# Retention and two feed-forward networks on one core: head tiles by pair, one weight piece ahead, ACT's table loaded first

## The chip, the cores and the metric

The kernel runs on one core of a Trainium2 chip. The time is device microseconds of one execution. Five engines work side by side, each on its own queue of instructions in order: PE multiplies matrices (PEld is its weight load), DVE and ACT do elementwise work, POOL does little here, and SP issues the transfers. An instruction that waits holds up everything behind it on its own engine.

## What is computed

The reference, cut to what matters. Four batches of eight heads go through a causal, decaying linear attention ("retention"), and the 2304 tokens that result through two networks.

```python
def _attn_ref(q, k, v):                      # 4 x 8 x 576 x 64
    scores = scale * np.matmul(q, k.transpose(0, 1, 3, 2))
    gamma = 1.0 - 2.0 ** (-5.0 - np.arange(H, dtype=np.float32))
    Dmat = np.where(rel >= 0, gamma[:, None, None] ** rel[None, :, :], 0.0)
    return np.matmul(scores * Dmat[None], v)

def _moe_ref(x, w1, w2, w3, w_out):          # x 2304 x 512
    return ((x @ w1) * (x @ w2) @ w3) @ w_out

def _moe2_ref(x, w_in, w_out, alpha):
    h = x @ w_in
    g = np.maximum(h, 0.0) + alpha * np.minimum(h, 0.0)
    return g @ w_out
```

## The kernel before

**Stages.** The retention of batch 0 comes first ("the heads"). Then the products of the first network, a = x @ w1 and b = x @ w2, run by blocks of 512 tokens, and the retention of the batches 1 to 3 is slipped in between them. Folded weights, the second product, the second network's hidden layer and its output follow; PE runs through those with few pauses, and no line of the change is in them.

**Retention.** Heads are taken in four pairs. A batch has one tile `qk` (queries and keys of all four pairs) and one tile `kv` (keys and values by chunk). `prep` (L246) scales the keys of a pair on ACT, two instructions a pair (L250). A step then handles one chunk of 128 tokens: PE makes the state product `st` (L272) and the scores `sc` (L276), DVE masks the scores (`rt`, L280) and carries the state `S` (L284 to L288), PE makes the output `o` from state and scores (L302, L310), DVE scales it (`xs`, L317), and ACT and DVE split it into a high and a low part, `xh` and `xl` (L169, L170), which the network multiplies. The last, half chunk has its own lines (L261, L263). Batch 0 is computed as two halves, pairs 0 and 1 (`r0`) and pairs 2 and 3 (`r1`), whose steps alternate in a list written out by hand (L380).

**Weights.** The weights come as float64 and are converted piece by piece by `Weights.tick` (L118), one stage a tick for each piece: ACT takes out two fields (L93, L94), DVE builds the float32 value from them in four instructions (L103, L104, L106, L108), ACT rounds it (L112), and DVE makes the rest (L116). `load_until` issues the transfers; five tiles `raw` hold pieces that are on their way. The heads tick at every second step, six times in all.

**Block 0 and batch 1.** An `ab_unit` (L401) does the two products of one column chunk: twelve matmuls (here called a unit) into `ps`, `cycle()`, twelve more, `cycle()`. A cycle runs the postponed work (`flush`), then steps of the next batch's retention at a given rate, then one tick. Before, batch 1's retention starts in the second of four `ab_unit`s and runs 7/6 steps a cycle. Block 1's first unit needs `xh` and `xl` of batch 1's chunk 3.

**Transfers.** SP issues all transfers in the order of the program. Batch 1's `qk` and `kv` go into the same two tiles as batch 0's, so each is one transfer, issued when PE has done with the heads (L391).

Of the kernel before, what the change touches and what calls it, by code (L numbers as in the profile page):

```python
# [7 lines left out]
F32 = mybir.dt.float32  # L8
# [8 lines left out]
P = 128  # L17
B, H, S, D = 4, 8, 576, 64
NPAIR = H // 2
NT, DM, DF1, DF2 = B * S, 512, 1024, 2048  # L20
CH = 128
# [114 lines left out]
def retention_moe_kernel(ctx: ExitStack, tc, qk, kv, w_out1, w3t, w12, w_in, w_out2, alpha, c_row, c_pair, out):  # L136
# [17 lines left out]

    idle = tmp.tile([P, 512], I32, tag="b", name="idle", bufs=2).bitcast(BF16)
    nc.vector.memset(idle, 0.0)

    later = []

# [77 lines left out]
    class Retention:  # L237
# [7 lines left out]

        def prep(self):  # L246
            for p in self.pairs:
                k = kvt[self.b][:, p]
                for j in range(2):
                    nc.scalar.activation(k[:, 4 * j:4 * j + 4], k[:, 4 * j:4 * j + 4], AF.Copy,  # L250
                                         scale=kd[:, 2 * p + j:2 * p + j + 1])

        def scores(self, c):
            b, n = self.b, self.n
            sc = self.psum["sc"].tile([P, 2, 512], F32, tag="sc", name=f"sc{b}_{c}")
            q, k, v = qkt[b][:, :, 0], qkt[b][:, :, 1], kvt[b]
            if c == NCH - 1:
                rt = self.rt[c] = attn.tile([P, NPAIR, 64], F32, tag="rte", name=f"rte{b}")[:, 0:n]
                for m, p in enumerate(self.pairs):
                    for pp in HEADS:  # L260
                        nc.tensor.matmul(sc[pp, 0, m * 64:(m + 1) * 64], k[pp, p, 512:S], q[pp, p, 512:S],  # L261
                                         start=True, stop=True, skip_group_check=True)
                later.append(lambda: nc.vector.tensor_tensor(  # L263
                    out=rt, in0=sc[:, 0, 0:64 * n].rearrange("p (n i) -> p n i", n=n), in1=mtail[:, self.ps],
                    op=ALU.mult))
                return
            i0 = c * CH
            rt = self.rt[c] = attn.tile([P, 2, NPAIR, CH], F32, tag="rt", name=f"rt{b}_{c}", bufs=2)[:, :, 0:n]
            st = self.psum["st"].tile([P, NPAIR, D], F32, tag="st", name=f"st{b}_{c}")[:, 0:n]
            for m, p in enumerate(self.pairs):  # L270
                for j, pp in enumerate(HEADS):
                    nc.tensor.matmul(st[pp, m], v[:, p, 4 * j + c], v[:, p, 8 + 4 * j + c],  # L272
                                     start=True, stop=True, skip_group_check=True)
            for m, p in enumerate(self.pairs):
                for j, pp in enumerate(HEADS):
                    nc.tensor.matmul(sc[:, j, m * CH:(m + 1) * CH], k[pp, p, i0:i0 + CH], q[pp, p, i0:i0 + CH],  # L276
                                     start=True, stop=True, skip_group_check=True)
# [12 lines left out]

            later.append(masked)

        def values(self, c):
            b, n = self.b, self.n
            w = CH if c < NCH - 1 else 64
            i0 = c * CH
            q, v, rt = qkt[b][:, :, 0], kvt[b], self.rt.pop(c)
            o = self.psum["o"].tile([P, NPAIR, CH], F32, tag="o", name=f"o{b}_{c}", bufs=2)
            if c:
                for m, p in enumerate(self.pairs):  # L300
                    for pp in HEADS:
                        nc.tensor.matmul(o[pp, m, 0:w], self.state[c - 1][pp, m], q[pp, p, i0:i0 + w],  # L302
                                         start=(m == 0), stop=False, skip_group_check=True)
            for m, p in enumerate(self.pairs):
                for j, pp in enumerate(HEADS):
                    if c < NCH - 1:
                        vj, rj = v[:, p, 8 + 4 * j + c], rt[:, j, m]
                    else:
                        vj, rj = v[pp, p, 16], rt[pp, m]
                    nc.tensor.matmul(o[pp, m, 0:w], vj, rj, start=(c == 0 and m == 0), stop=True,  # L310
                                     skip_group_check=True)
            later.append(lambda: self.decayed(c, o, w))
# [25 lines left out]
                return run  # L338
            return [step(c) for c in range(-1, NCH)]

    qkt, kvt = {}, {}

    def room_for(b):
        qkt[b] = attn.tile([P, NPAIR, 2, S], F32, tag="qk", name=f"qk{b}")
        kvt[b] = attn.tile([P, NPAIR, 17, D], F32, tag="kv", name=f"kv{b}")

    def load_batch(b):
        room_for(b)
        nc.sync.dma_start(out=qkt[b], in_=qk[b].rearrange("n p a s -> p n a s"))
        nc.sync.dma_start(out=kvt[b], in_=kv[b].rearrange("n p a d -> p n a d"))  # L350

    def load_pair(b, p):
        nc.sync.dma_start(out=qkt[b][:, p], in_=qk[b, p])
        nc.sync.dma_start(out=kvt[b][:, p], in_=kv[b, p])
        nc.sync.dma_start(out=per_pair[:, p], in_=c_pair[:, p])

    def attention_psum(stack, twice):
        return {"sc": pool(stack, f"ps_sc{twice}", bufs=twice, space=PSUM, reuse_waits="tile"),
# [3 lines left out]

    first = ExitStack()
    psum0 = attention_psum(first, 2)
    room_for(0)
    nc.sync.dma_start(out=per_row, in_=c_row)
    load_pair(0, 0)
    load_pair(0, 1)
    ws.load_until(2)
    load_pair(0, 2)  # L370
    load_pair(0, 3)
    ws.load_until(3)
    nc.sync.dma_start(out=al, in_=alpha)
    warm = psum0["o"].tile([P, 512], F32, tag="o", name="warm", bufs=2)
    for _ in range(16):
        nc.tensor.matmul(warm, idle[:, 0:P], idle[:, :512], start=True, stop=True)
    r0, r1 = Retention(0, [0, 1], psum0), Retention(0, [2, 3], psum0)
    r0.prep()
    s0, s1 = r0.steps(), r1.steps()
    order = [s0[0], s0[1], s0[2], s0[3], None, s1[0], s0[4], s1[1], s0[5], s1[2], s1[3], s1[4], s1[5]]  # L380
    for n, step in enumerate(order):
        if step is None:
            r1.prep()
            continue
        step()
        if n % 2:
            ws.tick()
        flush()
    flush()
    flush()  # L390
    load_batch(1)  # L391
    first.close()


# [52 lines left out]
    r = retention(1)  # L447
    for c in range(4):
        ws.until(2 * c + 2)
        ab_unit(0, c, cycle(r if c else None, 7 / 6))  # L450
    r.rest()
    flush()
    flush()
# [590 lines left out]
```

## Time and profile before

| | us |
|---|---|
| median of 3 runs | 832.91 (832.14 to 834.66) |
| the profiled execution | 832.39 |
| its span, first to last instruction | 830.6 |
| PE busy | 805.1 (97%) |
| DVE busy | 502.0 (60%) |
| ACT busy | 348.7 (42%) |

The 1.8 us between the profiled execution's time and its span lie before the first and after the last instruction. The shares are means over stages with different limits; the first 100 us look different from the rest, and the rows further down are from there. A row of the timeline gives start, duration, engine, line, operation, what it writes and reads, and in brackets how long the engine was idle before it and what ended that.

### The profile page before, as it was taken

How to read it: one execution, taken by the hardware profiler on the slowest of the kernel's cores; microseconds unless marked ns; L12 is line 12 of the kernel's file. 1: busy time of each engine (PE TensorE's matmuls, PEld its weight loads, DVE VectorE, ACT ScalarE, POOL GpSimd, SP SyncE). 2: the span in 40 equal slices, each digit the busy share in tenths (PEclk: the TensorE clock that was granted, in tenths of full speed). 3: DMA queues.
4: the chain of work that ended last, by engine and by line, in shares of the span. 5: the costliest groups of instructions: out<-in, count | busy, mean ns of one | idle time of the engine just before them, and what ended most of it. 6: DMA issues, size and time to landing. Idle time of an engine off the chain costs nothing.

```text
span 830.6 us, 12656 instructions
## 1 busy us (share of the span) xinstructions
PE 805.1 (97%) x4768; PEld 706.3 (85%) x4768; DVE 502.0 (60%) x887; ACT 348.7 (42%) x647; POOL 16.3 (2%) x12
## 2 busy tenths in 40 slices
PE   7889899999999999999999999999998999999998
PEld 4668688788888998899999998998996888888886
DVE  3869732633547769898780559769789943222222
ACT  3464423123135456655552446455566632222221
POOL 0000000000000000000010002102000000000000
PEclk9689899999999999999999999999999999999999
DMA  9383622145146657999962953433556725344341
GB/s 353 142 347 129 247 101 102 52 173 202 52 149 196 191 162 243 365 324 405 406 215 93 341 207 111 166 114 128 199 199 233 246 95 171 96 133 133 98 139 49
DMA packets 78557, 155.90 MB, mean 188 GB/s; under 512 B 7584, under 2 KB 55200, under 8 KB 78496
## 3 DMA queue, kind: packets, MB, share of 16 engines
q1 hardware_dynamic: 78496, 155.10, 52.2%
q8 instruction: 37, 0.61, 0.3%
q14 instruction: 24, 0.20, 0.1%
HBM read 103.69 MB, written 51.38 MB: 187 GB/s over the span
## 4 chain that ended last, share of the span: by engine, by line
PE 84%; DVE 7%; DMA 5%; issue 2%; ACT 1%; SPq 1%; ACTq 0%; DVEq 0%
PE o L959 22%; PE ps L176 22%; PE h L801 18%; PE y L735 12%; PE pw L550 5%; DMA kv<-in_kv_dram 2%; PE o L310 1%; PE sc L276 1%; DMA al<-in_alpha_dram 1%; PE st L272 1%; DMA raw<-in_w_dram 1%; DMA gr<-gd 1%; PE o L302 1%; DVE xB L692 1%; DVE a L106 1%
## 5 line engine op out<-in xcount | busy, mean ns | idle before, releaser
L176 PE MATMUL ps<-xh,w 128*128 128x512 f32 (+1 forms) x640 | 188.7, 376 | 2.7 <-ACT xh L169 2.7
L959 PE MATMUL o<-wb,gh 128*128 128x512 f32 x576 | 177.6, 389 | 1.1 <-ACT gh L169 1.1
L176 PEld LDWEIGHTS ps<-xh,w 128*128 128x128 f32 x640 | 117.9, 191 | 26.0 <-ACT xh L169 3.3
L959 PEld LDWEIGHTS o<-wb,gh 128*128 128x128 f32 x576 | 108.0, 188 | 23.7 <-ACT gh L169 1.5
L176 PE MATMUL ps<-xl,w 128*128 128x512 f32 (+1 forms) x320 | 119.6, 374 | 0.7 <-DVE xl L170 0.7
L959 PE MATMUL o<-wb,gl 128*128 128x512 f32 x288 | 112.3, 390 | 0.4 <-DVE gl L170 0.4
L170 DVE TENSOR_TENSOR gl<-gr,gh 128x768 fp32r<-128x768 f32 x48 | 46.0, 958 | 99.9 <-ACT gh L169 99.7
L735 PE MATMUL y<-yab,wp 128*128 128x384 f32 x576 | 100.0, 334 | 0.0
L735 PEld LDWEIGHTS y<-yab,wp 128*128 128x128 f32 x576 | 99.9, 188 | 0.1
L169 ACT CAST gh<-gr 128x768 fp32r<-128x768 f32 x48 | 40.2, 838 | 116.6 <-PE o L959 113.8
L176 PEld LDWEIGHTS ps<-xl,w 128*128 128x128 f32 x320 | 61.3, 192 | 11.2 <-DVE xl L170 1.3
L959 PEld LDWEIGHTS o<-wb,gl 128*128 128x128 f32 x288 | 54.1, 188 | 12.6 <-DVE gl L170 1.3
L813 DVE SCALAR_TENSOR_TENSOR g<-m,al,g 128x384 f32<-128x384 f32 x48 | 29.6, 617 | 48.5 <-ACT g L812 46.9
L801 PE MATMUL h<-xT,wv 128*128 128x384 f32 x288 | 55.1, 335 | 3.9 <-DVE g L819 3.9
L421 DVE TENSOR_TENSOR f<-f,ps 128x512 f32<-128x512 f32 (+1 forms) x40 | 25.3, 632 | 51.4 <-PE ps L176 51.1
L801 PE MATMUL h<-xT,wu 128*128 128x384 f32 x288 | 54.9, 334 | 0.3 <-ACT h L826 0.3
L801 PEld LDWEIGHTS h<-xT,wv 128*128 128x128 f32 x288 | 50.2, 188 | 4.9 <-DVE g L819 4.9
L417 ACT CAST ab<-f 128x512 fp32r<-128x512 f32 (+1 forms) x40 | 23.0, 576 | 71.4 <-DVE f L421 65.8
L108 DVE CUSTOM_DVE_ANT_0 a<-a,b 128x1024 uint16<-128x1024 uint16 x72 | 49.5, 688 | 3.2
L801 PEld LDWEIGHTS h<-xT,wu 128*128 128x128 f32 x288 | 50.3, 188 | 0.6 <-ACT h L826 0.6
L431 ACT COPY f<-ps 128x512 f32<-128x512 f32 (+1 forms) x40 | 21.7, 543 | 64.9 <-PE ps L176 64.7
L550 PE MATMUL pw<-wo,w 128*128 128x512 f32 x192 | 43.7, 389 | 0.0
(83 smaller groups left out, 1052.6 us busy)
## 6 DMA issues: line engine op xcount, KB each, us to landing
gd<-g SPq DMA_DIRECT2D x96, 192.0 KB, 1.9
gr<-gd SPq DMA_DIRECT2D x96, 192.0 KB, 2.5
abd<-ab SPq DMA_DIRECT2D x32, 512.0 KB, 2.6
raw<-in_w_out_dram SPq DMA_DIRECT2D x24, 512.0 KB, 3.9
yab<-abd SPq DMA_DIRECT2D x24, 384.0 KB, 8.3
raw<-in_w_dram SPq DMA_DIRECT2D x16, 512.0 KB, 7.7
raw<-in_w3t_dram SPq DMA_DIRECT2D x16, 512.0 KB, 4.1
rawi<-in_w_in_dram SPq DMA_DIRECT2D x16, 512.0 KB, 5.7
```

What stands on the lines that cost most here:

```text
L108: nc.vector.tensor_tensor(out=a.bitcast(I32), in0=a.bitcast(I32), in1=b, op=ALU.add)
L169: nc.scalar.copy(hi, src)
L170: nc.vector.tensor_tensor(out=lo, in0=src, in1=_f32(hi), op=ALU.subtract)
L176: nc.tensor.matmul(ps, a, bb, start=(n == 0), stop=(n == last))
L417: nc.scalar.copy(t[:, 0], f)
L421: nc.vector.tensor_tensor(out=f, in0=f, in1=pss[1], op=ALU.mult)
L431: later.append(product if m else (lambda: nc.scalar.copy(f, pss[0])))
L550: nc.tensor.matmul(acc[i], a[:, ic], bb, start=(k == 0 and n == 0), stop=(k == C1 - 1 and n == 2))
L735: nc.tensor.matmul(ys[o], wpc[c][a][:, oc], yab[b, c][:, bb], start=(c == 0 and i == 0), stop=(c == C1 - 1 and i == 2))
L801: nc.tensor.matmul(ps, a[:, x, ks], b[:, y, k], start=(fresh and n == 0), stop=(n == 5), skip_group_check=True)
L813: nc.vector.scalar_tensor_tensor(out=g, in0=r, scalar=neg[:, c:c + 1], in1=g, op0=ALU.mult, op1=ALU.add)
L959: nc.tensor.matmul(accs[b][i], x[:, m, ic], y, start=(j == 0 and m == 0 and q == 0), stop=(j == C1 - 1 and m == 1 and q == 2))
```

## The change

- **Tiles by pair.** `qk` and `kv` become four tiles each, one for each pair of heads, and every use takes its pair's tile. The loads of the batches 1 to 3 become eight transfers each. For batch 1 the pairs 0 and 1 are loaded when `r0` has issued its last step, the pairs 2 and 3 after the last step of `r1`.
- **A weight piece ahead.** The first piece's transfer is issued ahead of everything else, two more ahead of pairs 2 and 3, a fourth behind them. Two ticks stand ahead of the heads, one on each side of `r0.prep()`, so that the heads' six ticks are the third to the eighth.
- **ACT's table.** A copy of one column (`al[:, 0:1]` from the zeroed tile `idle`; `alpha` overwrites it later) is ACT's first instruction, and the table load stands before it.
- **Batch 1's retention** starts in the first `ab_unit` and runs one step a cycle.

```diff
     nc.vector.memset(idle, 0.0)
+    nc.scalar.copy(al[:, 0:1], idle[:, 0:1])
...
-    def load_batch(b):
-        room_for(b)
-        nc.sync.dma_start(out=qkt[b], in_=qk[b].rearrange("n p a s -> p n a s"))
-        nc.sync.dma_start(out=kvt[b], in_=kv[b].rearrange("n p a d -> p n a d"))
-
-    def load_pair(b, p):
-        nc.sync.dma_start(out=qkt[b][:, p], in_=qk[b, p])
-        nc.sync.dma_start(out=kvt[b][:, p], in_=kv[b, p])
-        nc.sync.dma_start(out=per_pair[:, p], in_=c_pair[:, p])
+    qkt, kvt = {b: {} for b in range(B)}, {b: {} for b in range(B)}
+
+    def load_pair(b, p):
+        qkt[b][p] = attn.tile([P, 2, S], F32, tag=f"qk{p}", name=f"qk{b}_{p}")
+        kvt[b][p] = attn.tile([P, 17, D], F32, tag=f"kv{p}", name=f"kv{b}_{p}")
+        nc.sync.dma_start(out=qkt[b][p], in_=qk[b, p])
+        nc.sync.dma_start(out=kvt[b][p], in_=kv[b, p])
+        if b == 0:
+            nc.sync.dma_start(out=per_pair[:, p], in_=c_pair[:, p])
+
+    def load_batch(b):
+        for p in range(NPAIR):
+            load_pair(b, p)
...
-    room_for(0)
+    ws.load_until(1)
     nc.sync.dma_start(out=per_row, in_=c_row)
     load_pair(0, 0)
     load_pair(0, 1)
-    ws.load_until(2)
+    ws.load_until(3)
     load_pair(0, 2)
     load_pair(0, 3)
-    ws.load_until(3)
+    ws.load_until(4)
...
+    ws.tick()
     r0.prep()
+    ws.tick()
...
         step()
+        if step is s0[-1]:
+            load_pair(1, 0)
+            load_pair(1, 1)
         if n % 2:
             ws.tick()
         flush()
     flush()
     flush()
-    load_batch(1)
+    load_pair(1, 2)
+    load_pair(1, 3)
...
-        ab_unit(0, c, cycle(r if c else None, 7 / 6))
+        ab_unit(0, c, cycle(r, 1))
```

How the instructions stand, at three places. In the names, a number behind a tile tells its use, and the lines of after are up to five higher than those of before.

DVE at the start of the heads, before, from its first work on batch 0 (`a` is a weight piece in conversion, `S`, `rt`, `xs` and `xl` belong to the heads):

```order
L284 COPY S_0_162<-st_0_152 128x128
L286 TENSOR_TENSOR S_1_187<-S_0_162,per_row 128x128
L280 TENSOR_TENSOR rt_0_151<-sc_0_150,per_pair 128x2x256
L103 TENSOR_SCALAR a_182<-a_182 128x512
L288 TENSOR_TENSOR S_1_187<-S_1_187,st_1_166 128x128
L104 TENSOR_SCALAR a_182<-a_182 128x512
```

The same place after, with the first piece's four instructions ahead of it:

```order
L103 TENSOR_SCALAR a_155<-a_155 128x512
L104 TENSOR_SCALAR a_155<-a_155 128x512
L106 SCALAR_TENSOR_TENSOR a_155<-raw_108,a_155 128x512
L108 ISA a_155<-a_155,b_156 128x1024
L285 COPY S_0_185<-st_0_175 128x128
L287 TENSOR_TENSOR S_1_216<-S_0_185,per_row 128x128
L103 TENSOR_SCALAR a_169<-a_169 128x512
L281 TENSOR_TENSOR rt_0_174<-sc_0_173,per_pair 128x2x256
L104 TENSOR_SCALAR a_169<-a_169 128x512
L289 TENSOR_TENSOR S_1_216<-S_1_216,st_1_189 128x128
L116 TENSOR_TENSOR w_0_205<-a_155,w_0_205 128x512
```

The first piece (`a_155`) is converted ahead of the heads; the second (`a_169`) stands between `S` and the first `rt`, where the first piece stood behind `rt`.

SP around the load of batch 1, before (`raw` is a weight piece, `abd` a product that is put away):

```order
L85 DMA raw_448<-in_w_dram 128x512
L349 DMA qk_479<-in_qk_dram 128x4x1152
L350 DMA kv_480<-in_kv_dram 128x4x1088
L85 DMA raw_514<-in_w_dram 128x512
L85 DMA raw_541<-in_w_dram 128x512
```

And after:

```order
L85 DMA raw_361<-in_w_dram 128x512
L347 DMA qk_0_391<-in_qk_dram 128x1152
L348 DMA kv_0_392<-in_kv_dram 128x1088
L347 DMA qk_1_395<-in_qk_dram 128x1152
L348 DMA kv_1_396<-in_kv_dram 128x1088
L85 DMA raw_425<-in_w_dram 128x512
L85 DMA raw_489<-in_w_dram 128x512
L347 DMA qk_2_520<-in_qk_dram 128x1152
L348 DMA kv_2_521<-in_kv_dram 128x1088
L347 DMA qk_3_524<-in_qk_dram 128x1152
L348 DMA kv_3_525<-in_kv_dram 128x1088
L85 DMA raw_567<-in_w_dram 128x512
```

The two transfers have become eight, in two groups with two weight pieces between them.

ACT from the first unit of block 0 on, before (`f` is a product taken from PE, `w` a rounded weight piece):

```order
L431 COPY f_0_498<-ps_0_0_500 128x512
L112 CAST w_4_517<-a_393 128x512
L93 ACTIVATE a_523<-raw_328 128x512
L94 ACTIVATE b_524<-raw_328 128x512
L112 CAST w_5_544<-a_457 128x512
L93 ACTIVATE a_550<-raw_384 128x512
L94 ACTIVATE b_551<-raw_384 128x512
L417 CAST ab_0_499<-f_0_498 128x512
L431 COPY f_1_554<-ps_1_0_556 128x512
L250 ACTIVATE kv_480<-kv_480,per_row 128x256 x8
L112 CAST w_6_582<-a_523 128x512
```

And after:

```order
L436 COPY f_0_543<-ps_0_0_545 128x512
L251 ACTIVATE kv_0_392<-kv_0_392,per_row 128x256 x2
L251 ACTIVATE kv_1_396<-kv_1_396,per_row 128x256 x2
L251 ACTIVATE kv_2_521<-kv_2_521,per_row 128x256 x2
L251 ACTIVATE kv_3_525<-kv_3_525,per_row 128x256 x2
L112 CAST w_6_570<-a_434 128x512
```

The keys' scaling has moved two units up, to directly behind the first unit's copy, and waits for each pair by itself.

## Rows read from the trace of the kernel before

**Rows 1.** The page's chain of work that ended last, by engine.

```profile
PE 84%; DVE 7%; DMA 5%; issue 2%; ACT 1%; SPq 1%; ACTq 0%; DVEq 0%
```

**Rows 2.** Stretches: start:end, length, busy us of PE, PEld, DVE, ACT, POOL, granted clock, DMA.

```profile
10.00:20.00 10.00, 8.56 (x100) 6.87 (x100) 7.37 (x19) 4.03 (x9) 0.00 (x0) 0.83 1.03 419
...
11.50:26.40 14.90, 12.79 (x146) 10.25 (x144) 11.65 (x29) 6.67 (x14) 0.00 (x0) 0.77 0.94 375
...
30.00:40.00 10.00, 8.53 (x92) 6.24 (x88) 9.47 (x24) 4.25 (x9) 0.00 (x0) 0.67 0.29 107
...
60.30:92.00 31.70, 29.03 (x323) 23.35 (x322) 30.42 (x56) 15.24 (x29) 0.00 (x0) 0.93 0.33 119
```

**Rows 3.** Timeline, the start of the heads on ACT and DVE.

```profile
7.09 1.28 ACT L250 ACT_TABLE_LOAD   x1 [7.09 <-DMA kv<-in_kv_dram]
...
8.39 0.91 ACT L250 ACTIVATE kv<-kv,per_row 128x256 f32<-128x256 f32 x2
...
10.34 0.91 ACT L250 ACTIVATE kv<-kv,per_row 128x256 f32<-128x256 f32 x2 [1.05 <-DMA kv<-in_kv_dram]
...
11.67 0.29 DVE L284 COPY S<-st 128x128 f32<-128x128 f32 x1 [10.27 <-PE st L272]
```

**Rows 4.** Groups by line, DVE from 60 to 92 us: busy us, mean ns.

```profile
L116 DVE TENSOR_TENSOR w<-a,w 128x512 fp32r<-128x512 f32 x6 | 4.1, 683 | 0.0
L108 DVE CUSTOM_DVE_ANT_0 a<-a,b 128x1024 uint16<-128x1024 uint16 x5 | 3.4, 687 | 0.3
...
L103 DVE TENSOR_SCALAR a<-a 128x512 f32<-128x512 f32 x6 | 2.5, 420 | 0.0
```

**Rows 5.** Transfers up to 62 us: count, KB each, median us from issue to landing.

```profile
qk<-in_qk_dram SPq DMA_DIRECT2D x1, 2304.0 KB, 8.7
...
kv<-in_kv_dram SPq DMA_DIRECT2D x1, 2176.0 KB, 14.4
```

**Rows 6.** Timeline, the load and the first step of batch 1.

```profile
41.58 0.38 SPq L349 DMA_DIRECT2D qk<-in_qk_dram  x1
...
56.51 3.30 ACT L250 ACTIVATE kv<-kv,per_row 128x256 f32<-128x256 f32 x8 [4.42 <-DMA kv<-in_kv_dram]
...
60.38 0.42 DVE L284 COPY S<-st 128x256 f32<-128x256 f32 x1 [5.40 <-PE st L272]
...
62.28 0.79 PE L176 MATMUL ps<-xh,w 128*128 128x512 f32 x1
```

**Rows 7.** Timeline, PE: one unit of block 0 and one step of batch 1.

```profile
75.39 0.50 PE L176 MATMUL ps<-xh,w 128*128 128x512 f32 x1
...
78.34 0.69 PE L272 MATMUL st<-kv 128*64 128x64 f32 x16
78.95 1.16 PE L276 MATMUL sc<-qk 64*128 64x128 f32 x16
...
82.09 0.50 PE L176 MATMUL ps<-xh,w 128*128 128x512 f32 x1
```

**Rows 8.** Timeline, DVE's last `xl` ahead of block 1, then PE's first matmuls of it.

```profile
91.38 1.09 DVE L170 TENSOR_TENSOR xl<-xs,xh 128x256 fp32r<-128x256 f32 x3
...
90.69 0.49 PE L176 MATMUL ps<-xh,w 128*128 128x512 f32 x1 [2.00 <-ACT xh L169]
91.86 0.79 PE L176 MATMUL ps<-xl,w 128*128 128x512 f32 x1 [0.67 <-DVE xl L170]
...
99.85 0.39 PE L176 MATMUL ps<-xh,w 128*128 128x512 f32 x1
```

**Rows 9.** The chain of waits in order of time, a piece of block 1: start, us.

```profile
139.00 7.48 PE ps L176 x33
```

**Rows 10.** Stretches of 1 us, columns as in rows 2.

```profile
57.00:58.00 1.00, 0.93 (x5) 0.71 (x6) 0.00 (x0) 1.00 (x4) 0.00 (x0) 0.55 1.04 381
...
91.00:92.00 1.00, 0.33 (x2) 0.14 (x1) 1.00 (x3) 0.31 (x1) 0.00 (x0) 0.61 0.92 248
...
98.00:99.00 1.00, 1.00 (x6) 0.84 (x5) 0.91 (x2) 1.00 (x3) 0.00 (x0) 0.97 1.02 422
```

More of the change, by code (lines that the diff above doesn't have):

```diff
@@ L247, in prep @@
             for p in self.pairs:
-                k = kvt[self.b][:, p]
+                k = kvt[self.b][p]
                 for j in range(2):
@@ L255, in scores @@
             sc = self.psum["sc"].tile([P, 2, 512], F32, tag="sc", name=f"sc{b}_{c}")
-            q, k, v = qkt[b][:, :, 0], qkt[b][:, :, 1], kvt[b]
+            qk, v = qkt[b], kvt[b]
             if c == NCH - 1:
@@ L260, in scores @@
                     for pp in HEADS:
-                        nc.tensor.matmul(sc[pp, 0, m * 64:(m + 1) * 64], k[pp, p, 512:S], q[pp, p, 512:S],
+                        nc.tensor.matmul(sc[pp, 0, m * 64:(m + 1) * 64], qk[p][pp, 1, 512:S], qk[p][pp, 0, 512:S],
                                          start=True, stop=True, skip_group_check=True)
@@ L271, in scores @@
                 for j, pp in enumerate(HEADS):
-                    nc.tensor.matmul(st[pp, m], v[:, p, 4 * j + c], v[:, p, 8 + 4 * j + c],
+                    nc.tensor.matmul(st[pp, m], v[p][:, 4 * j + c], v[p][:, 8 + 4 * j + c],
                                      start=True, stop=True, skip_group_check=True)
@@ L275, in scores @@
                 for j, pp in enumerate(HEADS):
-                    nc.tensor.matmul(sc[:, j, m * CH:(m + 1) * CH], k[pp, p, i0:i0 + CH], q[pp, p, i0:i0 + CH],
+                    nc.tensor.matmul(sc[:, j, m * CH:(m + 1) * CH], qk[p][pp, 1, i0:i0 + CH], qk[p][pp, 0, i0:i0 + CH],
                                      start=True, stop=True, skip_group_check=True)
@@ L296, in values @@
             i0 = c * CH
-            q, v, rt = qkt[b][:, :, 0], kvt[b], self.rt.pop(c)
+            qk, v, rt = qkt[b], kvt[b], self.rt.pop(c)
             o = self.psum["o"].tile([P, NPAIR, CH], F32, tag="o", name=f"o{b}_{c}", bufs=2)
@@ L301, in values @@
                     for pp in HEADS:
-                        nc.tensor.matmul(o[pp, m, 0:w], self.state[c - 1][pp, m], q[pp, p, i0:i0 + w],
+                        nc.tensor.matmul(o[pp, m, 0:w], self.state[c - 1][pp, m], qk[p][pp, 0, i0:i0 + w],
                                          start=(m == 0), stop=False, skip_group_check=True)
@@ L306, in values @@
                     if c < NCH - 1:
-                        vj, rj = v[:, p, 8 + 4 * j + c], rt[:, j, m]
+                        vj, rj = v[p][:, 8 + 4 * j + c], rt[:, j, m]
                     else:
-                        vj, rj = v[pp, p, 16], rt[pp, m]
+                        vj, rj = v[p][pp, 16], rt[pp, m]
                     nc.tensor.matmul(o[pp, m, 0:w], vj, rj, start=(c == 0 and m == 0), stop=True,
@@ L339, in steps @@
             return [step(c) for c in range(-1, NCH)]
[L341 to L345, printed above, removed]
-    def load_batch(b):
-        room_for(b)
-        nc.sync.dma_start(out=qkt[b], in_=qk[b].rearrange("n p a s -> p n a s"))
-        nc.sync.dma_start(out=kvt[b], in_=kv[b].rearrange("n p a d -> p n a d"))
-    def load_pair(b, p):
-        nc.sync.dma_start(out=qkt[b][:, p], in_=qk[b, p])
-        nc.sync.dma_start(out=kvt[b][:, p], in_=kv[b, p])
-        nc.sync.dma_start(out=per_pair[:, p], in_=c_pair[:, p])
+    qkt, kvt = {b: {} for b in range(B)}, {b: {} for b in range(B)}
[6 more added lines that the diff above has]
+            nc.sync.dma_start(out=per_pair[:, p], in_=c_pair[:, p])
+    def load_batch(b):
+        for p in range(NPAIR):
+            load_pair(b, p)
     def attention_psum(stack, twice):
```

## The prediction, made blind

> **What bounds the kernel now.** I read the page's chain first: PE carries 84% of the span [rows 1], so only what stops or slows PE counts. Then the table of stretches, for where PE isn't at its full pace, and the timeline there. All that the change touches lies ahead of about 100 us, in three pieces.
>
> The heads, from 11.67 us [rows 3] to 41.58, where SP may overwrite their tiles [rows 6]. PE's work there is small; DVE is busy for 9.47 of 10 us between 30 and 40 [rows 2] and sets the pace. Earlier it has room: 11.65 of 14.9 us between 11.5 and 26.4 [rows 2].
>
> The load of batch 1. It is issued at 41.58 and `kv` is there for ACT at 56.51, after a wait of 4.42 us; PE's state products follow ACT's eight scalings (3.30 us) one by one, DVE waits 5.40 us for them and starts at 60.38, and the next unit of block 0 starts at 62.28 [rows 6].
>
> From there to block 1, PE and DVE are both full: DVE 30.42 of 31.7 us [rows 2]; PE runs without a pause until 88.69, then waits 2.00 and 0.67 us for the last `xh` and `xl` [rows 8]. The waits have a second price: the granted clock is 0.55 of full (mostly 1.2 instead of 2.4 GHz) as PE starts on batch 1, it falls again at 91 and is back at 98 [rows 10]. The first 24 matmuls of block 1 take from 90.69 to 99.85 + 0.39 = 100.24 [rows 8], 9.55 us; at the pace of 33 matmuls in 7.48 us [rows 9] they would take 5.44. The excess of 4.1 us is 0.67 of wait and 3.4 of low clock.
>
> **The change part by part.** I follow the new order to the end of block 1's first 24 matmuls; behind them PE runs on as before, so what is won there reaches the end.
>
> *The table load.* It costs 1.28 us at 7.09, between the landing of the first pair and its scaling at 8.39 [rows 3]. Ahead of the heads it lies under the first transfers and costs nothing: 1.28 us won on ACT.
>
> *The first piece's transfer.* It goes ahead of the pairs: 512 KB at 419 GB/s [rows 2] take 1.25 us. For the first pair this eats what the table load gives back, so scaling starts near 8.4 as before. The second pair had its scaling at 10.34, 1.05 us of it waiting for its transfer and none of it for the table [rows 3]; it comes 1.25 later, less up to 0.4 as the transfers start one issue earlier. I take 1.0: `S` at 12.7 instead of 11.67. The piece's ACT work (two instructions) and its four on DVE (L103 and L104 0.42 each, L106 and L108 0.69 each, 2.2 us [rows 4]) lie in front of that, in idle time, and cost nothing.
>
> *Two ticks more ahead of the end of the heads.* A tick brings DVE these four (2.2 us) and one L116 of 0.68 [rows 4]. With one set of four hidden, the heads hold one set more and two L116 more: 2.2 + 1.4 = 3.6 us. Against that stand 14.9 - 11.65 = 3.25 us of idle DVE [rows 2]. Bound below: all of it is filled and the heads end only the 1.0 us later. Bound above: none is, since idle moments between dependent instructions can't be used, and they end 1.0 + 3.6 = 4.6 later. The new order speaks for the middle (the second piece's L103 now stands ahead of the first `rt` and waits for ACT and a transfer there, while later pieces fill gaps): 1.0 + 1.6 = 2.6. The heads end at 44.2 instead of 41.58. This is the cost of the change.
>
> *Pair by pair.* Pairs 0 and 1 of batch 1 are issued once `r0` is through, some 10 us ahead of the heads' end, and land under the rest. Queued behind them on SP are two weight pieces, needed later. What remains at 44.2 are pairs 2 and 3, 2.3 MB instead of 4.6. The 2304 KB of `qk` took 8.7 us from issue to landing [rows 5], so I take that and 0.2 for four issues instead of one: 53.1. PE meanwhile has two units of 78.34 - 75.39 = 2.95 us [rows 7] and the same waits at the first of them, some 2 us: it is through at about 52, ahead of the landing. ACT scales pairs 0 and 1 while it waits, and then only the last pair, 0.91 us [rows 3]. What is queued on ACT behind that wait is the next tick and the high part of the first product; DVE waits for them too, as it does before from 55 to 60. With 0.4 for the last state products, `S` of batch 1 starts at 54.4 instead of 60.38, and the scores (79.0 to 80.1 in a later step, 1.1 us [rows 7]) end at 55.5 instead of 62.28.
>
> *From there to block 1.* Before, PE went from 62.28 to 88.69 with four units and the five remaining steps, 26.4 us. Now six units are left, since the retention starts two units earlier: 2 x 2.95 more [rows 7], less 0.7 for the first unit before, which ran at the low clock: 31.6 us, hence 87.1. DVE's way there: from `S` at 60.38 to the last `xl`, 91.38 + 0.2, took 31.2 us [rows 6, 8]. By the new order the content of this stretch is the same plus one L108 of 0.69 [rows 4]; the two extra ticks stand behind the `xl`, because the retention now ends a cycle ahead of the units. 54.4 + 31.9 = 86.3. So PE finds `xl` ready with 0.8 us to spare, and the waits of 2.00 and 0.67 us and the low clock behind them go. What is late next is PE itself.
>
> *Sum.* The 24 matmuls end at 87.1 + 5.44 + 0.2 = 92.7 instead of 100.24: 7.5 us won at full clock. PE has a short pause left, from about 52 to 54. At the longer pause before batch 1 the clock fell [rows 6, 10]; at this one it may. One low stretch of 7 us cost 3.4 us in block 1; here the dense work follows at once, and I charge 1.5, between nothing and 3.4. **7.5 - 1.5 = 6.0 us.** The profiled execution took 832.39, which gives 826.4; it lies 0.5 under the median of 832.91, against which I set 826.9. The loads of batches 2 and 3 get eight issues of 0.38 [rows 6] instead of two; they are needed tens of microseconds later and cost nothing.
>
> **A rule weighed.** In the trace, transfers of 0.2 to 0.6 MB queued behind each other moved 419 GB/s from 10 to 20 us [rows 2], as fast as larger ones. The Trainium skill (DMA: Bandwidth & Descriptors, section Bandwidth) asks for transfers of 1 MiB and more and measures 341 GB/s at 1 MB: smaller loads would lose. By its figure the 2.3 MB would need an estimated 1.3 us more, and the sum would be 4.7; by the row nothing.
>
> **The rivals.**
> *The wait comes back.* With 0.8 us between DVE's 86.3 and PE's 87.1, a DVE that is 1 us slower makes PE wait at block 1 again, and the clock falls with it: up to 2.0 + 0.67 + 3.4 = 6.1 us, about 832. For it: DVE was 96% busy there [rows 2]. Against: before, `xl` came 2.7 us behind PE, and two units now stand between.
> *The early load isn't early.* If SP stands at a weight piece's wait until the heads end, all four pairs move behind 44.2 and land 14.4 us on [rows 5], at 58.6. The gain shrinks by 5.5 to about 832.5. Against: the pieces queued ahead of it reuse tiles whose work on DVE is done by about 26.
> *Small transfers are slow.* The rule above as a mechanism: the last pair lands 1.3 us later and everything behind it; 828.2.
> *The low clock stays*, the case that ends slower. Between 30 and 40 us PE held 0.67 of full clock although 8.5 of 10 us busy [rows 2], because small products alternate with waits for DVE. If the pause at 52 brings the low level and the tightly coupled steps of batch 1 hold it, the 31.6 us run at half pace for a while. Each microsecond of low level costs half; with 7.5 to lose, it turns to a loss beyond 15 us. Held for the whole stretch, the work of 31.6 us takes up to twice that; held for half of it, some 16 are lost: about 841. Against it: before, the clock came back within this same mix. The Trainium skill (TensorE: Matmul & The Clock Gate, section What's actually happening) calls the low level the default, which activity releases; rows 10 agree in that it falls at pauses.
>
> **How the numbers follow.** A difference of about 0.3%, 2.5 us, is what a measurement here can tell from none. The forecast has 0.72, the wait that comes back 0.10, the load that isn't early 0.06, small transfers 0.05, the low clock 0.07. The forecast's own bounds: 1.0 instead of 2.6 for the heads and no low clock, 9.1 us won, 823.8; 4.6 for the heads and 3.4 for the clock, 2.1 won, 830.8. Small transfers lie inside; the two cases at 832 and the slow one stay out, 0.23, so I widen the range a little, 823.5 to 831.5. Faster: the forecast but for 0.02 at its edge, and small transfers, 0.75. Same: that edge and the two cases at 832, 0.18. Slower: 0.07.
>
> **What would show it.** The heads end (batch 1's pair 2 issued) between 42.6 and 46.2, best 44.2. ACT's first scaling at 8.4. `kv` of the last pair landed near 53, `S` of batch 1 at 54.4. Block 1's first matmul near 87, with no wait over 0.5 us ahead of it, and its 24 matmuls in 5.5 us at clock 1.00. It is wrong if the heads end behind 47, if PE waits for `xl` at block 1, or if the clock is under 0.9 between 60 and 85.

## The result, and the profile after

The changed kernel took 827.96 us (median of 6 runs, 825.38 to 829.24), the kernel before 834.51 on the same chip in the same job (6 runs). The ratio is 0.9915, 95% interval 0.9887 to 0.9943: about 0.85% faster, 6.6 us by the medians. The profiled execution of after took 828.57 us with a span of 826.8, against 832.39 and 830.6 before: 3.8 us. So there are two differences for one change: 6.6 us by the medians of six runs each, and 3.8 us between two single executions, which the traces below account for.

The page's chain that ended last, by engine, after (before: [rows 1]):

```profile
PE 88%; DVE 5%; DMA 3%; issue 2%; ACT 1%; SPq 1%; ACTq 0%; DVEq 0%
```

PE's share went from 84 to 88%, taken from DVE and DMA. The start of the heads in the timeline after (start us, duration, engine, line, what; in brackets the idle time ahead and what ended it), to be read beside [rows 3]:

```profile
9.07 0.91 ACT L251 ACTIVATE kv<-kv,per_row 128x256 f32<-128x256 f32 x2 [3.73 <-DMA kv<-in_kv_dram]
...
12.32 0.91 ACT L251 ACTIVATE kv<-kv,per_row 128x256 f32<-128x256 f32 x2 [2.35 <-DMA kv<-in_kv_dram]
...
13.80 0.29 DVE L285 COPY S<-st 128x128 f32<-128x128 f32 x1 [6.53 <-PE st L273]
```

The table load is gone from there, but each pair now waits for its own transfer, and comes 0.7 and 2.0 us later; DVE's first `S` comes 2.1 later, at 13.80 instead of 11.67.

The load and first step of batch 1, timeline after, beside [rows 6]:

```profile
33.17 0.33 SPq L347 DMA_DIRECT2D qk<-in_qk_dram  x1
...
45.44 0.33 SPq L347 DMA_DIRECT2D qk<-in_qk_dram  x1
...
53.98 0.91 ACT L251 ACTIVATE kv<-kv,per_row 128x256 f32<-128x256 f32 x2 [1.09 <-DMA kv<-in_kv_dram]
54.54 0.73 PE L273 MATMUL st<-kv 128*64 128x64 f32 x4 [1.27 <-ACT kv L251]
...
55.30 0.42 DVE L285 COPY S<-st 128x256 f32<-128x256 f32 x1 [1.92 <-PE st L273]
...
56.29 0.50 PE L177 MATMUL ps<-xh,w 128*128 128x512 f32 x1
```

Pair 0 of batch 1 is issued at 33.17, pair 2 at 45.44, when the heads end (3.9 later than before). The last pair is there at 53.98, `S` starts at 55.30 instead of 60.38, the next unit at 56.29 instead of 62.28.

Block 1: first the chain of waits in order of time (start, us, what), then DVE's `xl` in the timeline, both after:

```profile
84.96 54.63 PE ps L177 x240
```

```profile
85.84 0.75 DVE L171 TENSOR_TENSOR xl<-xs,xh 128x256 fp32r<-128x256 f32 x2
```

Before, PE stood 2.00 and 0.67 us ahead of block 1 for `xh` and `xl` [rows 8]. Now the last unit of block 0 (12 matmuls) and block 1 are one stretch, 0.2276 us a matmul: block 1 starts at 84.96 + 12 x 0.2276 = 87.7, and its 24 matmuls end at 93.2 instead of 100.24. `xl` is ready at 86.6, 1.1 us ahead of PE. The stretches after (start:end, length, busy us of PE, PEld, DVE, ACT, POOL, granted clock, DMA share, GB/s), beside [rows 2, 10]:

```profile
0.00:10.00 10.00, 6.62 (x18) 2.34 (x18) 2.72 (x5) 3.60 (x6) 0.20 (x4) 1.00 0.76 262
11.50:26.40 14.90, 11.01 (x106) 8.67 (x106) 11.71 (x29) 7.66 (x16) 0.00 (x0) 0.70 0.99 398
...
48.00:58.00 10.00, 8.66 (x60) 6.80 (x59) 4.34 (x10) 7.31 (x16) 0.00 (x0) 1.00 0.76 286
55.30:87.50 32.20, 32.20 (x343) 25.90 (x344) 31.47 (x59) 17.87 (x33) 0.00 (x0) 1.00 0.35 119
...
91.00:92.00 1.00, 1.00 (x6) 0.85 (x5) 1.00 (x3) 1.00 (x3) 0.00 (x0) 1.00 1.01 417
```

From 48 to 92 us the rows show the clock at full speed, through PE's pause of 1.27 us ahead of 54.54 and through the place at 91 us where it stood at 0.61 before. From 55.3 to 87.5 PE is busy without a gap.

**A milestone besides the time.** Behind block 1, PE runs on to the second product of the first network without another decision of this change. Its start in the chain of waits is 347.52 before and 340.63 after: 6.9 us, nearly what block 1 showed (7.1). The rest of the 3.8 against 6.9 lies at the end. The chain's late pieces, before:

```profile
347.52 98.32 PE y L735 x567
...
637.60 3.85 DMA gr<-gd
...
643.42 183.45 PE o L959 x808
```

and after:

```profile
340.63 98.32 PE y L740 x567
...
630.87 5.08 DMA gr<-gd
...
637.93 185.05 PE o L964 x808
```

PE at the entry of the last stage in the timeline, first before, then after:

```profile
642.43 0.73 PE L959 MATMUL o<-wb,gh 128*128 128x512 f32 x2 [1.08 <-ACT gh L169]
```

```profile
636.93 0.73 PE L964 MATMUL o<-wb,gh 128*128 128x512 f32 x2 [2.45 <-ACT gh L170]
```

There PE waits for a tile that goes out to memory and back. From the second product's start to the last piece it took 297.3 instead of 295.9, 1.2 of these 1.4 in the transfer shown, and the last piece itself 1.60 longer at equal instructions, because the clock fell: 0.57 of full between 638 and 642, 1.00 before. Together that is the missing 3.0. No line of the change is there, and in e2 and e3, whose instructions there are the same, the transfer took 3.95 and 4.09 and the last piece 183.46; the section on the hardware comes back to this. So each run is judged below by its median and by the start of the second product.

The second product's start is from one execution of each kernel, and it still holds what the clock did behind block 1's first wait. The chain's piece there, with equal work, before and in e6:

```profile
91.86 54.62 PE ps L176 x227
```

```profile
95.61 51.75 PE ps L177 x227
```

In e6 the clock did not fall. In before it fell, which cost 2.9 us in this piece, and e4, e7 and e10 lie between with 53.3. The same kernel in two executions, e1 and e12, differs by 0.9 without any such fall. Differences at the second product are read with these two numbers in mind.

### The profile page after: what moved, and what is told of

The parts are those of the page before. It is cut to its first block, busy times and chain, and to the rows that moved or that the text cites. A ratio compares the mean times of both kernels' runs of the same rounds, so it can differ in the third digit from the quotient of the medians.

```text
span 826.8 us, 12692 instructions
## 1 busy us (share of the span) xinstructions
PE 801.9 (97%) x4768; PEld 704.2 (85%) x4768; DVE 502.4 (61%) x887; ACT 349.8 (42%) x648; POOL 16.2 (2%) x12
## 4 chain that ended last, share of the span: by engine, by line
PE 88%; DVE 5%; DMA 3%; issue 2%; ACT 1%; SPq 1%; ACTq 0%; DVEq 0%
PE ps L177 24%; PE o L964 22%; PE h L806 19%; PE y L740 12%; PE pw L555 5%; PE o L311 2%; PE sc L277 2%; PE o L303 1%; DMA gr<-gd 1%; DMA raw<-in_w_dram 1%; DMA kv<-in_kv_dram 1%; PE st L273 1%; DVE xB L697 1%; DVE a L106 1%; DVE g L824 0%
## 5 line engine op out<-in xcount | busy, mean ns | idle before, releaser
L177 PE MATMUL ps<-xh,w 128*128 128x512 f32 (+1 forms) x640 | 186.8, 373 | 0.0
```

The costliest lines, as they stand in the source:

```text
L177: nc.tensor.matmul(ps, a, bb, start=(n == 0), stop=(n == last))
```

## The experiments

Times in us; "heads end" is the issue of batch 1's first transfer that has to wait for all heads (pair 2 with tiles by pair), "second product" its start in the chain. The ratio is taken from all runs and not from the two medians, so they can differ by up to 0.2%.

| kernel | median (before, same job) | ratio, 95% | heads end | `S` of batch 1 | second product |
|---|---|---|---|---|---|
| before | 834.51 | 1 | 41.58 | 60.38 | 347.52 |
| after | 827.96 (834.51) | 0.9915, 0.9887 to 0.9943 | 45.44 | 55.30 | 340.63 |
| e1_no_piece | 821.34 (833.90) | 0.9865, 0.9841 to 0.9889 | 41.07 | 51.08 | 336.38 |
| e2_no_table | 826.54 (833.90) | 0.9924, 0.9899 to 0.9949 | 45.45 | 55.40 | 340.70 |
| e3_load_late | 826.45 (833.90) | 0.9920, 0.9896 to 0.9944 | 45.66 | 55.54 | 340.83 |
| e4_start_late | 830.56 (833.90) | 0.9977, 0.9958 to 0.9997 | 45.84 | 60.96 | 345.71 |
| e5_whole_tiles | 838.08 (834.37) | 1.0038, 1.0016 to 1.0060 | 46.39 | 64.05 | 351.12 |
| e6_piece_alone | 839.40 (834.37) | 1.0066, 1.0044 to 1.0088 | 45.25 | 63.77 | 348.40 |
| e7_tiles_alone | 826.06 (834.37) | 0.9916, 0.9886 to 0.9947 | 41.55 | 55.82 | 340.60 |
| e8_five_ticks | 825.27 (834.37) | 0.9900, 0.9873 to 0.9927 | 42.29 | 51.97 | 337.26 |
| e9_alpha_early | 823.29 (833.47) | 0.9880, 0.9859 to 0.9901 | 40.35 | 49.76 | 335.05 |
| e10_before_alpha | 831.44 (833.47) | 0.9978, 0.9960 to 0.9997 | 40.56 | 59.36 | 345.50 |
| e11_alpha_no_table | 823.19 (834.25) | 0.9884, 0.9864 to 0.9904 | 40.40 | 49.61 | 334.90 |
| e12_no_piece_again | 823.40 (834.25) | 0.9890, 0.9867 to 0.9912 | 41.05 | 50.15 | 335.46 |

My theory of the change: tiles by pair and the earlier start of batch 1's retention win, by ending the wait for the load and then the wait at block 1; the early piece only costs; the table is covered anyway. Rivals: the piece pays for itself later, since weights come earlier; or the win comes from the place of the load calls.

**e1_no_piece**: after without the early piece.

```diff
-    ws.load_until(1)
     nc.sync.dma_start(out=per_row, in_=c_row)
-    ws.load_until(3)
+    ws.load_until(2)
-    ws.load_until(4)
+    ws.load_until(3)
-    ws.tick()
     r0.prep()
-    ws.tick()
```

> The changed kernel without the weight piece ahead: the first piece's transfer and the two ticks are back where they were; tiles by pair, the early load, the early start of batch 1 and the table load stay. Theory (the piece and its ticks are the whole cost of the change and bring nothing back, because the work on DVE from batch 1's first S to the last xl is the same with and without them): the heads end near 41.5 us instead of 45.4, batch 1's S comes near 51.4 instead of 55.3, block 1 starts near 83.6 instead of 87.5, and the kernel is 3 to 4 us faster than the changed one, about 8 to 11 under the kernel before. Rival (the pieces converted ahead pay for themselves in block 0, where DVE is full): PE waits for xl or w ahead of block 1, and the time is that of the changed kernel or above it.

The heads end at 41.07, 4.4 earlier than in after, and the second product starts 4.25 earlier; e12, the same kernel in another job, 5.2 earlier. The chain at block 1 shows no wait either:

```profile
80.71 54.63 PE ps L177 x240
```

The early piece is a loss, and nothing up to block 1 gives it back. The version without it beats both kernels.

**e2_no_table**: after without the copy.

```diff
-    nc.scalar.copy(al[:, 0:1], idle[:, 0:1])
```

> The changed kernel without the copy that puts ACT's table load first. Theory (the table load is worth nothing, since ACT's first work is now the early weight piece, 5 us ahead of the first pair): the load comes at the piece's landing near 4 us, the first scaling stays at 9.1, the heads end at 45.4, and the time is the changed kernel's, within 0.3%. Rival (the load was worth its 1.28 us): everything 1.3 us later.

The second product starts at 340.70, as in after. I had expected the load at 4 us, ahead of the piece's first instruction. ACT's timeline in e2 has it at the very start:

```profile
0.73 1.28 ACT L93 ACT_TABLE_LOAD   x1 [0.73 <-PEq L1031]
4.01 0.66 ACT L93 ACTIVATE a<-raw 128x512 f32<-128x512 f32 x1 [2.00 <-DMA raw<-in_w_dram]
```

The load belongs to L93, but it does not wait for the piece that L93 waits for. In before it stood at 7.09, behind a wait for `kv` [rows 3]. What decides this difference was not tried. Beside the piece, the copy is worth nothing.

**e3_load_late**: all eight transfers of batch 1 behind the heads in the program.

```diff
-        if step is s0[-1]:
-            load_pair(1, 0)
-            load_pair(1, 1)
...
-    load_pair(1, 2)
-    load_pair(1, 3)
+    load_batch(1)
```

> The changed kernel with all eight transfers of batch 1 issued after the heads. Theory (the gain comes from having only two pairs to load after the heads): heads end at 45.4 as in the changed kernel, the last pair lands near 60 instead of 54, S near 61.3, block 1 starts near 93.6, some 6 us later than in the changed kernel, and with the longer pause the clock falls, up to 3.4 us more: 834 to 837. Rival (the gain comes from starting batch 1's retention earlier in the units, not from the load): the time of the changed kernel, near 828.

The expectation missed: 340.83, as in after. SP's own timeline in e3:

```profile
36.92 0.80 SPq L85 DMA_DIRECT2D raw<-in_w_dram  x2
37.83 0.37 SPq L347 DMA_DIRECT2D qk<-in_qk_dram  x1
...
45.66 0.33 SPq L347 DMA_DIRECT2D qk<-in_qk_dram  x1
```

Pair 0 goes out at 37.83, still 8 us ahead of the heads' end. SP reaches the calls early, since it does nothing but issue; what holds a transfer back is its tile, and pair 0's is free when `r0` is through. So the tiles by pair make the load early; the place of the calls moved pair 0 by 4.7 us (33.17 in after) and the second product by 0.2. e5 tests the tiles.

**e4_start_late**: batch 1's retention starts one unit later, as before.

```diff
-        ab_unit(0, c, cycle(r, 1))
+        ab_unit(0, c, cycle(r if c else None, 7 / 6))
```

> The changed kernel with batch 1's retention started in the second of the four units at 7/6 steps a cycle, as before. Theory (after the load DVE is the limit: from S to the last xl it takes 31 us whatever PE does, so what counts is when S can start): PE does four units without a pause until about 58, S comes near 59 instead of 55.3, the last xl near 90, PE waits some 4 us ahead of block 1 and the clock falls there; 4 to 7 us over the changed kernel, 832 to 835. Rival (PE is the limit, and a start without the pause is better): block 1 starts near 85.7, 1.8 us earlier than in the changed kernel, 826.

The load is early here too, but ACT's scaling stands at 57.23 without a wait, behind the second unit's work, and `S` comes at 60.96. PE at block 1 in e4:

```profile
90.17 0.50 PE L177 MATMUL ps<-xh,w 128*128 128x512 f32 x1 [2.33 <-ACT xh L170]
91.33 0.79 PE L177 MATMUL ps<-xl,w 128*128 128x512 f32 x1 [0.66 <-DVE xl L171]
```

and the stretch behind it, where the clock is at half (1.2 GHz):

```profile
92.00:94.00 2.00, 2.00 (x6) 1.57 (x5) 0.55 (x1) 0.00 (x0) 0.00 (x0) 0.50 0.96 364
```

Both waits and the low clock are back: 5.1 us later at the second product. As the theory had it, the early start is what ends the wait at block 1. The size is less sure: the profiled execution, 834.79, is the second slowest of ten, and the median of 830.56 lies below the 832 to 835 expected, 2.6 us over after's by the medians of two jobs and 0.6% by the ratios.

**e5_whole_tiles**: after with one `qk` and one `kv` tile a batch, and one transfer each. Apart from indices:

```diff
-        qkt[b][p] = attn.tile([P, 2, S], F32, tag=f"qk{p}", name=f"qk{b}_{p}")
-        kvt[b][p] = attn.tile([P, 17, D], F32, tag=f"kv{p}", name=f"kv{b}_{p}")
+        qkt[b] = attn.tile([P, NPAIR, 2, S], F32, tag="qk", name=f"qk{b}")
+        kvt[b] = attn.tile([P, NPAIR, 17, D], F32, tag="kv", name=f"kv{b}")
```

> The changed kernel with one qk and one kv tile for a batch, as before, so that batch 1 is two transfers that wait for the end of the heads; the early weight piece, the table load and the early start stay. Theory (the tiles by pair are what makes the load early, wherever the program issues it): heads end near 45.5, kv lands near 60.4 instead of 54.0, S comes near 64.3 instead of 55.3, block 1 starts near 97 instead of 87.5 and the clock falls in the longer pause: 9 to 13 us over the changed kernel, 837 to 841, slower than the kernel before. Rival (the gain comes from the earlier start of batch 1's retention): 831 or less.

ACT and DVE in e5, timeline:

```profile
60.18 3.30 ACT L251 ACTIVATE kv<-kv,per_row 128x256 f32<-128x256 f32 x8 [7.95 <-DMA kv<-in_kv_dram]
...
64.05 0.43 DVE L285 COPY S<-st 128x256 f32<-128x256 f32 x1 [8.89 <-PE st L273]
```

Without the tiles the change loses: the heads' later end goes straight into the load, ACT waits 7.95 us instead of 4.42 [rows 6], and the second product starts 3.6 later than before. Started early without its data, the retention waits longer. Whether the early start still helps a little without the tiles stays open: against e6, the same kernel without it, the median is 1.3 us lower, the second product 2.7 later.

**e6_piece_alone**: before with the piece, its two ticks and the table.

> The kernel before with the early weight piece, its two ticks and the table load, and nothing else. Theory (they cost what the heads end later, and nothing gives it back): heads end near 45.5 instead of 41.6, everything behind it 3.9 us later, 838. Rival (two pieces converted ahead shorten what DVE has to do ahead of block 1): the wait ahead of block 1 shrinks from 2.7 us and the time is that of the kernel before, 834.

The heads end at 45.25, 3.7 later than before, and the ratio is 0.66% above 1, as the theory said. In the profiled run, the fastest of ten at 834.99, PE starts block 1 at 94.44, 3.75 later than before, and the second product only 0.9 later: the waits there shrank from 2.7 to 1.9 us (1.21 and 0.66), and the clock did not fall behind them, which gave 2.9 back.

**e7_tiles_alone**: after without the piece, the table and the early start; that is, e1's diff, e2's and e4's together.

> The kernel before with the tiles by pair alone: no early piece, no table load, batch 1's retention started as before. Theory (DVE needs 31 us from S to the last xl, and S follows the second unit pair of block 0): heads end near 41.1, the last pair lands near 50, S comes near 56.3 after four units instead of 60.4, PE waits 2 to 3 us ahead of block 1, which starts near 86 instead of 90.7; 4 to 5 us under the kernel before, 829. Rival (with the early load the start of the retention doesn't matter): as the run without the piece, 821.

It came out between theory and rival. PE at block 1 in e7:

```profile
85.04 0.50 PE L176 MATMUL ps<-xh,w 128*128 128x512 f32 x1 [2.34 <-ACT xh L169]
86.20 0.50 PE L176 MATMUL ps<-xl,w 128*128 128x512 f32 x1 [0.66 <-DVE xl L170]
```

The wait is the old one, only 5.6 us earlier. The tiles alone give 6.9 us at the second product, as much as the whole change; 1.3 of it is a shorter low clock behind the wait (53.35 for the 227 matmuls, 54.62 before). The early start adds 4.2 on top (e7 to e1, which also has the copy for the table), by ending the wait and the low clock, and the early piece takes 4.25 away again (e1 to after).

**e8_five_ticks**: e1 with one tick less in the heads.

```diff
-        if n % 2:
+        if n % 2 and n < 11:
```

> The run without the early piece, with five ticks instead of six among the heads (the last one left to block 0). Theory (DVE sets the pace of the heads, so a tick less there is 2.2 + 0.7 us less of its work, and the work between S and the last xl stays as it is): heads end near 38.8 instead of 41.1, everything behind it 2 to 2.5 us earlier, 819. Rival (the weights come too late for block 0's units then, each w one cycle later): PE waits for w in block 0, and the time is 821 or more.

The heads did not get shorter: 42.29 against 41.07. Two things stand in the trace. The sixth tick's work on DVE starts at 41.38 in e1 (an L116, then L103 at 41.99), behind the last instruction that the heads' end needs, so there was nothing to save. And DVE stood longer, by 1.6 us, at an instruction that I had not looked at. DVE's timeline, first e1, then e8:

```profile
21.79 0.18 DVE L782 TENSOR_SCALAR al<-al 128x16 f32<-128x16 f32 x1 [0.94 <-DMA al<-in_alpha_dram]
```

```profile
22.99 0.18 DVE L782 TENSOR_SCALAR al<-al 128x16 f32<-128x16 f32 x1 [2.54 <-DMA al<-in_alpha_dram]
```

The edit does not reach that place: up to there the order is that of e1 and e12, alpha's load is issued at 13.5 to 13.8 us in all three, and the wait was 0.94, 0.46 and 2.54 us; it differs from execution to execution. The rival's mechanism is not in the trace either, since PE never waits for `w` in block 0; but its time is, 825.27, and 3.9 us over e1's median (of another job) are accounted for at the second product with 0.9 only. The rest stays open.

The instruction makes the negative of `alpha`, which is needed only in the second network; but the order puts it into the heads, and alpha's 8 KB are issued behind three weight pieces. Before has it too, and after has the same instruction, one tick later, without a wait. First before, then after:

```profile
22.17 0.17 DVE L780 TENSOR_SCALAR al<-al 128x16 f32<-128x16 f32 x1 [1.74 <-DMA al<-in_alpha_dram]
```

```profile
24.51 0.17 DVE L785 TENSOR_SCALAR al<-al 128x16 f32<-128x16 f32 x1
```

**e9_alpha_early**: e1 with alpha's load behind the first pair. **e10_before_alpha**: before with the same edit.

```diff
     load_pair(0, 0)
+    nc.sync.dma_start(out=al, in_=alpha)
     load_pair(0, 1)
...
-    nc.sync.dma_start(out=al, in_=alpha)
```

> The kernel of e1 with the small load of alpha issued behind the first pair instead of behind the third weight piece. In e1, before, e7 and e8 DVE stands 0.9 to 2.5 us in the middle of the heads at the one instruction that needs alpha (0.94 in e1, 1.74 in before, 2.54 in e8); in after that instruction stands one tick later and does not wait. Theory: this wait is on the path, so the heads end 0.9 earlier than in e1 (40.1 instead of 41.07 us) and the second product starts at 335.4 instead of 336.4; the median is 0.9 to 1.5 under e1's 821.3. Rival: DVE then waits for the products instead, the heads end at 41 as in e1, no difference. Second rival: the small load ahead of the second pair delays that pair's scaling beyond 11.5 us and the first S behind 13, and eats the gain.

> The kernel before with the same move of alpha's load alone. Theory: the wait of 1.74 us at the instruction on alpha goes, the heads end at 39.9 instead of 41.58, everything up to block 1 comes as much earlier, and the second product starts at 345.8 instead of 347.5: 1.7 us faster than the kernel before in the same job. It would also say that the two ticks of the change cost more than the heads' later end shows, since in after this wait is gone too. Rival: the time is taken up by another wait, no difference.

In e10 the instruction stands at 7.88 us, in idle time, the heads end 1.0 earlier, PE starts block 1 at 89.95, 0.7 earlier, and the second product starts 2.0 earlier. The other 1.3 are a shorter low clock behind block 1's wait (53.33 us for the 227 matmuls, 54.62 before), which the two executions do not tie to alpha. The ratio is 0.22% under 1 (0.03 to 0.40%). In e9 the heads end 0.7 earlier than in e1 and e12, the second product 1.3 earlier than in e1 and 0.4 earlier than in e12, the same kernel; by the medians they can't be told apart.

**e11_alpha_no_table**: e9 without the table's copy (e2's diff). **e12_no_piece_again**: e1's kernel beside it.

> The kernel of e9 (tiles by pair, retention of batch 1 one unit earlier, alpha's load early, no early piece) without the copy that brings ACT's table in first. Theory: the table load stands at 7.1 us again, the first pair's scaling at 8.4 instead of 7.1, but the second pair is scaled at 10.4 as in e9, because it waits for its transfer, and the first S stays at 11.8: nothing is lost, the second product starts at 335 us and the median equals e9's and lies 0.9 to 1.3 under e12 of the same job. Rival: the table is worth its 1.28 us, the first S comes at 13 and the second product at 336.3.

> The kernel of e1 unchanged, beside e11 on the same chip, since the medians of e1 and e9 come from two jobs: second product at 336.4 us, median 821 to 823. If alpha's early load is worth what e9's trace showed, this one is 0.9 to 1.3 us slower than e11; if the two agree within 0.3, the early load is worth nothing that lasts.

ACT in e11, timeline:

```profile
7.13 1.28 ACT L250 ACT_TABLE_LOAD   x1 [7.13 <-DMA kv<-in_kv_dram]
8.42 0.91 ACT L250 ACTIVATE kv<-kv,per_row 128x256 f32<-128x256 f32 x2
10.40 0.91 ACT L250 ACTIVATE kv<-kv,per_row 128x256 f32<-128x256 f32 x2 [1.08 <-DMA kv<-in_kv_dram]
```

The table load delays the first pair by 1.3, the second pair waits for its transfer as ever, and the first `S` comes at 11.88 (e9: 11.83). So the table's place moves nothing behind the first pair, with or without the piece. e11's second product starts 0.56 ahead of e12's, but the medians, 823.19 and 823.40, do not show it. Which of e1, e9 and e11 is best stays open; all three lie under after, by 4.7 to 6.6 us in the medians of different jobs and by 4.3 to 5.7 at the second product.

## Why the prediction was right, and where its steps were off

The forecast of 826.9 and the range held the time; the sign and the mechanism were right, some terms were not. That 826.9 lies so near 827.96 is partly luck: the heads ended 1.2 later than forecast, and the 1.5 charged for the clock, which were not due, covered it.

*The first piece's transfer: mis-sized.* I took 1.25 us at the 419 GB/s of 10 to 20 us [rows 2], and 1.0 net at `S`. It cost 2.1, and ACT's first scaling came at 9.07, not at 8.4. The transfer runs in the first ten microseconds, where the page's rates are lower; the kernel before, in the same columns as above:

```profile
0.00:10.00 10.00, 6.46 (x20) 2.43 (x20) 0.48 (x1) 2.19 (x3) 0.20 (x4) 1.00 0.79 283
```

At that rate 512 KB take an estimated 1.85 us, at after's 262 GB/s 2.0; the second pair lost 2.0 (10.34 to 12.32). Both rates are means that include a start of about 2 us with next to nothing moved. What the trace shows directly is that after moved 190 GB/s from 3 to 5 us and before 332; why is not shown. The row to take was that of the stretch in which the transfer stands.

*The two ticks: right size, wrong account.* The stretch from the first `S` to the heads' end, before and after, in the same columns:

```profile
11.67:41.58 29.91, 25.27 (x280) 19.52 (x280) 25.76 (x64) 12.43 (x26) 0.00 (x0) 0.71 0.58 225
```

```profile
13.80:45.44 31.64, 25.56 (x274) 19.73 (x276) 29.07 (x71) 15.13 (x31) 0.00 (x0) 0.72 0.78 298
```

DVE had 3.3 us more to do, and the stretch took 1.7 more. I had said 1.6, as the middle between full cover and none. But 1.74 us of the idle DVE time that I counted as possible cover was the wait for alpha. With alpha early (e10: 40.56 - 11.91) the same stretch takes 28.65 with 25.70 of DVE work, so the ticks cost 3.0, near my bound without cover of 3.6, and the vanished wait paid 1.3 of it back. A list of what ended DVE's idle time there would have shown this before.

*The heads' end* therefore came at 45.44, not 44.2, within the bounds of 42.6 to 46.2.

*The table: right in the sum, wrong in the reason.* I let the piece eat a gain of 1.28; e11 shows that there was none, as the second pair's transfer sets `S`.

*Pair by pair: right.* The last pair was there 8.5 us behind the heads' end (forecast 8.9), and `S` stood at 55.30; the forecast was 54.4, with the heads' end 1.2 earlier. The load is early because of the tiles, as the prediction had it; e3 shows in addition that the calls' place hardly matters. The Trainium skill (DMA: Bandwidth & Descriptors, section Bandwidth) asks for large transfers, and I weighed a charge of 1.3 us by its figure. The landing does not show it, but the rates show a part; first before, with large transfers, then after, with those by pair:

```profile
46.00:56.00 10.00, 8.18 (x37) 6.43 (x35) 7.30 (x13) 4.98 (x9) 0.00 (x0) 1.00 1.02 420
```

```profile
47.00:54.00 7.00, 6.27 (x35) 4.84 (x33) 2.68 (x6) 3.71 (x10) 0.00 (x0) 0.94 1.00 369
```

On the 2.3 MB of two pairs that is an estimated 0.8 us. It is not tied to the size alone: e11 moved the same transfers at 408 GB/s (42 to 48 us).

*Block 1: right.* DVE needed 31.3 us from `S` to the end of the last `xl` (forecast 31.9), PE came at 87.7 (87.1), 1.1 to spare (0.8). Of the 7.1 us won here, 3.0 are the earlier start, 0.67 a wait and 3.4 the clock; e6 shows that this clock is not lost in every execution. e4 shows the wait that I named as a rival coming back as soon as the retention starts one unit later. I priced that rival at up to 6.1 us and wrote 832; 826.9 and 6.1 are 833.0.

*The clock: a charge that was not due.* I charged 1.5 for a fall at the pause around 53 us, which I took for 2 us long; it was 1.27, and the clock did not fall. Without that charge the sum was 7.5, and 7.1 came at block 1, 6.9 at the second product. That the profiled executions differ by 3.8 only is 3.0 lost at 631 to 642, which no step of mine named.

*What I did not see:* the early piece is worth less than nothing. I priced it at 2.6 and called it "the cost of the change" without asking what it buys; e1 and e12 say nothing, at 4.25 to 5.2 us.

## What to carry to other kernels

Here a transfer into a reused buffer went out once the buffer's last reader was done, so tiles of the size in which work finishes made the load early, with its call early or late (issued at 33.17 or 37.83 us; with whole tiles at 46.39). Ask of each part of a change what it buys as well as what it costs: here the tiles and the early start won 11 us together, and the piece gave 4 to 5 of it back. Idle time of a busy engine is cover only when it is not itself a wait for something; and the cost of a transfer is read from the rates of its own stretch. A milestone in one trace leaves out what happens behind it, but not what the clock did ahead of it: look there before a difference of 1 to 3 us is given to a change.

## What the runs showed of the hardware

**Equal work, in steps of 1.6 us.** The second network's three long stretches `h` and the stage behind it have the same instructions in all these kernels. The chain's pieces in e9, from the second `h` on (the first took 49.17, in e11 49.19):

```profile
497.61 49.17 PE h L803 x282
557.92 52.28 PE h L803 x300
...
630.96 183.45 PE o L961 x808
```

and in e11:

```profile
497.48 50.76 PE h L802 x282
559.38 53.88 PE h L802 x300
...
634.13 183.48 PE o L960 x808
```

Two of e11's are 1.6 us longer. The clock there, first e9, then e11:

```profile
496.00:500.00 4.00, 2.75 (x17) 2.43 (x16) 3.96 (x8) 1.08 (x3) 0.00 (x0) 1.00 0.28 102
```

```profile
496.00:500.00 4.00, 2.75 (x12) 2.52 (x11) 3.97 (x9) 0.96 (x3) 0.00 (x0) 0.77 0.28 102
```

PE pauses equally long in both: it waits 1.25 us for DVE ahead of 497.61 in e9 and of 497.48 in e11, and is busy for 2.75 of the 4 us. In one the clock falls and in the other it does not. It explains how e11, ahead of e12 at the second product, can be behind it in the profiled run's time, and why a change of 1 us can hide in a median of six.

**At the entry of the last stage the longer wait went with the fall.** The last piece is 1.6 us longer in after too (185.05 against 183.45), but there PE had not paused equally: the wait for `gh` was 2.45 us in after and 1.08 before. In all fourteen kernels it comes out the same way: where this wait was 1.99 to 2.65 us (after, e4, e5, e8) the last piece took 185.0 to 185.6, where it was 0.99 to 1.49 (the other ten) 183.5.

**Elsewhere a wait of that length did not decide it.** PE's waits for batch 1's keys of 1.27 us in after and 2.24 in e8 left the clock at 1.00. At block 1, waits of 2.00 and 0.67 us before, 2.33 and 0.66 in e4, 2.34 and 0.66 in e7 and 1.31 and 0.66 in e10 were followed by half the clock; 1.21 and 0.66 in e6 were not. What decides it was not found.
